# Batch 0's attention reordered by head halves in a fused pooled-attention and MLP kernel

## The chip, the cores and the metric

The kernel runs on one core of one Trainium2 chip. Its time is the device time of one launch in microseconds, as the median of several runs. The kernel before takes 300.92 us (three runs, 300.75 to 301.02). The profile is of one execution; its span, from the first to the last instruction, is 299.0 us.

## The reference

Eight batches of eight heads, 576 tokens and 64 values per head. Keys and values are averaged over groups of eight tokens, so that 72 pooled keys remain. The queries attend to these, and the result goes through a layer with `h - tanh(h)` between two weight matrices.

```python
# q, k, v: (8, 8, 576, 64) float32; w_in: (512, 2048); w_out: (2048, 512)
k_p = k.reshape(B, H, 72, 8, D).mean(axis=3)
v_p = v.reshape(B, H, 72, 8, D).mean(axis=3)
scores = scale * np.matmul(q, k_p.transpose(0, 1, 3, 2))
attn = softmax(scores)
attn_out = np.matmul(attn, v_p)                       # (8, 8, 576, 64)
x = attn_out.transpose(0, 2, 1, 3).reshape(4608, 512)
h = x @ w_in
return (h - np.tanh(h)) @ w_out                       # (4608, 512) float32
```

## The kernel before

The tokens of the second part are worked off in nine groups of 512. Group 0 needs only the first 512 tokens of batch 0. While TensorE works on a group, the other engines prepare the attention of the next batch. Two things are special at the start: nothing can be multiplied with the weights until batch 0's attention is there, and batch 1's attention is computed between the products of group 0.

Names: `k_raw`, `v_raw`, `v_bf` and `q_bf` are loaded or cast inputs; pooled keys of two heads (144 rows) fill one tile of 128 rows, and the 16 rows left over of each of the four pairs are collected in a fifth tile (index `NM`). `KB` holds the pooled keys turned, `qT` the queries turned, `E` the exponentials of the scores, `VB` the pooled values with a column for the denominator, `x0` and `xT` the attention result before and after turning, `gT` is `h - tanh(h)`.

The loads at the start, on three queues (SyncE, ScalarE, GpSimd):

```python
load_main(k_pairs, k_raw[0], 0, 0, 1)      # nc.sync
load_q0(0, 2)                              # nc.scalar
load_main(k_pairs, k_raw[0], 0, 1, 2)
load_q0(2, 4)
load_main(k_pairs, k_raw[0], 0, 2, 4)
load_q0(4, 8)
load_dense(k_pairs, k_raw[0], 0, nc.scalar)   # leftover keys
load_dense(v_pairs, v_raw[1], 0, nc.scalar)   # leftover values
warm_pe(9)                                    # products of zeros on TensorE
...
nc.gpsimd.memset(q_bf[64:128, R, :, :], 0.0)
... # mask
for i in range(2):
    nc.gpsimd.tensor_scalar_mul(VB[i][:, :, D:D1], mask[:, :, :], float(POOL))
nc.gpsimd.dma_start(out=v_bf[:, 0:NM, :], in_=v_pairs[0, 0:128, :, :])   # casts to bf16
... # spread
for c in range(4):
    load_w1(c)                                # casts to bf16
load_w2(0)
nc.gpsimd.tensor_copy(out=v_bf[:, NM, :], in_=v_raw[1][:, NM, :])
load_w2(1)
... # three memsets
after(load_k(1), w1_dmas[1])                  # starts when that quarter of w1 has landed
load_q(1, False)
load_main(v_pairs, v_raw[1], 1, 0, NM)
```

Batch 0's attention, in the order of TensorE's queue:

```python
pool_k(0, nc.vector, 0, 1)
pool_k(0, nc.vector, 1, 2)
q_turn(nc.scalar.copy, 0, 2)                  # cast of q to bf16
q_turn(nc.scalar.copy, 2, 4)
k_turn(0, 1)
q_pe_transpose(0, (0,), "act")
warm_pe(1)
k_turn(1, 2)
q_pe_transpose(0, (1,), "act")
warm_pe(2)
scores_wide(0, (0, 1))                        # product and exponential
...                                           # load of the last 64 queries
q_turn(nc.scalar.copy, 4, 6)
q_turn(nc.scalar.copy, 6, 8)
pool_k(0, nc.vector, 2, 4)
warm_pe(6)
k_turn(2, 4)
pool_k(0, nc.vector, NM, NT)                  # leftover keys
warm_pe(2)
q_pe_transpose(0, (2, 3), "act")
warm_pe(2)
scores_wide(0, (2, 3))
k_turn_left()
warm_pe(2)
v_ps = v_pe_pool(NM, NT, spread)              # values are pooled by TensorE
scores_wide(0, (NM,))
v_left(VB[0], v_ps[:, 0, :, :], nc.vector)
vs = v_pe_pool(0, NM, ident, 4)
v_main(VB[0], vs, nc.vector, 0, 2)
v_main(VB[0], vs, nc.vector, 2, 4)
...
warm_pe(2, b0=3)
av_pair(0, 0, 2)                              # token blocks 0, 1; heads 0 to 3
av_pair(1, 0, 5)                              # blocks 2, 3
av_pair(0, 1, 0)                              # heads 4 to 7
warm_pe(1)
x0_turn((0, 1), 0, 7, nc.scalar.copy)
av_pair(1, 1, 2)
warm_pe(1)
x0_turn((2, 3), 0, 5, nc.scalar.copy)
warm_pe(2)
h_open(3, 4)                                  # first half of the sum of one tile of h
x0_turn((0, 1), 1, 7, nc.scalar.copy)
h_open(0, 0)
h_open(1, 1)
x0_turn((2,), 1, 5, nc.scalar.copy)
x0_turn((3,), 1, 6, nc.vector.tensor_copy)
h_open(2, 2)
h_open(4, 3)
...
for i in range(5):
    mlp_h_mms(0, i, 2, 4)                     # second half of the sum
    mlp_h_act(i, gts)                         # tanh on ScalarE, h - tanh on VectorE
for i in range(5, NHID):                      # NHID = 16
    mlp_h(0, i, gts)
    ...                                       # i == 7, 9, 11, 13: the last 64 tokens of batch 0
pool_k(1, nc.gpsimd, mid=(2, 3))              # load_w2(2), load_w2(3) after the first addition
after(load_k(2), w2_dmas[2])
...
for u in range(16):
    mlp_o(0, u % 4, u // 4 * 4, u // 4 * 4 + 4, gts, o_pools[u % 4])   # four products with w2
    ...                                       # u == 2: turn batch 1's keys; u == 3: its queries
```

`av_pair` includes the normalization: a reciprocal and a product on VectorE.

Of the kernel before, what the change touches and what calls it, by code (L numbers as in the profile page):

```python
# [19 lines left out]
R = 4  # L20
# [17 lines left out]
def kernel(  # L38
# [41 lines left out]
    ps_h = Banks(0, 1, 2)  # L80
    ps_o = Banks(3, 4)
    ps_a = Banks(5, 6, 7)
# [25 lines left out]
    rot = [0]  # L108

    def ps_any(shape, dtype, name):  # L110
        pool, tag = [(ps_a, "ps_a"), (ps_h, "hT_ps")][rot[0] % 2]
        rot[0] += 1
        return pool.tile(shape, dtype, name=name, tag=tag)
# [40 lines left out]
    def load_q(b, tail=True):  # L154
        if b not in q_raws:
            q_raws[b] = raw.tile([128, H, R + 1, D], FP32, name="q_raw", tag="q_raw")
        t = q_raws[b]
        nc.sync.dma_start(
            out=t[:, :, 0:R, :], in_=q[b, :, 0:QA, :].rearrange("h (p j) d -> p h j d", j=R)
        )  # L160
        if tail:
            load_q_tail(b, t, nc.sync)

# [3 lines left out]
    def q_cast(b, eng=nc.gpsimd.tensor_copy, parts=1):  # L167
# [7 lines left out]
        eng(out=q_bf[:QT, R, :, :], in_=t[:QT, :, R, :])  # L175
# [75 lines left out]
    def v_main(vb, vs, eng, t0, t1):  # L251
# [3 lines left out]
            in0=vs[:, t0:t1, :, :].to_broadcast([128, n, 2, D]),  # L255
# [192 lines left out]
    def mlp_h_mms(g, i, f0, f1, pool=None):  # L448
# [3 lines left out]
        for fb in range(f0, f1):  # L452
# [5 lines left out]
                stop=(fb == NFB - 1),  # L458
            )
# [101 lines left out]

    nc.vector.memset(zeros, 0.0)  # L562
# [6 lines left out]
    load_main(k_pairs, k_raw[0], 0, 2, 4)  # L569
    load_q0(4, 8)  # L570
    load_dense(k_pairs, k_raw[0], 0, nc.scalar)
    load_dense(v_pairs, v_raw[1], 0, nc.scalar)

    warm_pe(9)
    nc.vector.memset(warm[:, :], 0.0)
    nc.scalar.activation(out=warm[:, :], in_=warm[:, :], func=ACT.Exp)
    nc.vector.memset(KB[0][:, :], 0.0)

    make_identity(nc, ident)
    nc.gpsimd.memset(q_bf[64:128, R, :, :], 0.0)  # L580
# [16 lines left out]
    for i in range(2):  # L597
        nc.gpsimd.tensor_scalar_mul(VB[i][:, :, D:D1], mask[:, :, :], float(POOL))
    nc.gpsimd.dma_start(out=v_bf[:, 0:NM, :], in_=v_pairs[0, 0:128, :, :])  # L599
# [5 lines left out]
    for c in range(4):  # L605
        load_w1(c)
    load_w2(0)
    nc.gpsimd.tensor_copy(out=v_bf[:, NM, :], in_=v_raw[1][:, NM, :])
    load_w2(1)
    nc.gpsimd.memset(k_raw[1][:, NM, :], 0.0)  # L610
    nc.gpsimd.memset(v_raw[0][:, NM, :], 0.0)
    nc.gpsimd.memset(KB[1][:, :], 0.0)

    q_raws[1] = raw.tile([128, H, R + 1, D], FP32, name="q_raw", tag="q_raw")
    after(load_k(1), w1_dmas[1])
    load_q(1, False)
    load_main(v_pairs, v_raw[1], 1, 0, NM)

    def k_turn(ta, tb):
        ps = ps_any([128, tb - ta, 128], FP32, "kT_ps")  # L620
        for t in range(ta, tb):
            turn_tile(ps[:, t - ta, :], kdups[0], t)
        kb_main(KB[0], ps, ta, tb, (nc.vector.tensor_copy, nc.vector.tensor_copy))

    def k_turn_left():
        ps = ps_any([128, 128], FP32, "kT_ps")
        turn_tile(ps[:, :], kdups[0], NM)
        kb_left(KB[0], ps, nc.vector.tensor_copy)

    pool_k(0, nc.vector, 0, 1)  # L630
    pool_k(0, nc.vector, 1, 2)
# [21 lines left out]

    q_turn(nc.scalar.copy, 0, 2)
    q_turn(nc.scalar.copy, 2, 4)
    k_turn(0, 1)
    q_pe_transpose(0, (0,), "act")
    warm_pe(1)
    k_turn(1, 2)
    q_pe_transpose(0, (1,), "act")  # L660
    warm_pe(2)
    scores_wide(0, (0, 1))
    nc.scalar.dma_start(out=t0[:QT, :, R, :], in_=q[0, :, QA:S, :].rearrange("h p d -> p h d"))
    q_turn(nc.scalar.copy, 4, 6)
    q_turn(nc.scalar.copy, 6, 8)
    pool_k(0, nc.vector, 2, 4)
    warm_pe(6)
    k_turn(2, 4)
    pool_k(0, nc.vector, NM, NT)
    warm_pe(2)  # L670
    q_pe_transpose(0, (2, 3), "act")
    warm_pe(2)
    scores_wide(0, (2, 3))
    k_turn_left()
    warm_pe(2)
    v_ps = v_pe_pool(NM, NT, spread)
    scores_wide(0, (NM,))
    v_left(VB[0], v_ps[:, 0, :, :], nc.vector)
    vs = v_pe_pool(0, NM, ident, 4)
    v_main(VB[0], vs, nc.vector, 0, 2)  # L680
    v_main(VB[0], vs, nc.vector, 2, 4)
    load_left(v_pairs, v_raw[1], 1, nc.scalar)
    load_q_tail(1, q_raws[1], nc.scalar)
    gts = []

    def av_pair(p, half, b0):
        ps = PS[:, b0 : b0 + 2, 0 : 4 * D1].rearrange("p k (h d) -> p k h d", d=D1)
        for k in range(2):
            av_mms(0, 2 * p + k, half, ps[:, k, :, :])
        rden = work.tile([128, 2, 4, 1], FP32, name="rden2", tag="rden2")  # L690
# [26 lines left out]
    def h_open(i, b0):  # L717
        mlp_h_mms(0, i, 0, 2, bank(b0, [128, TG]))

    warm_pe(2, b0=3)  # L720
    av_pair(0, 0, 2)
    av_pair(1, 0, 5)
    av_pair(0, 1, 0)
    warm_pe(1)
    x0_turn((0, 1), 0, 7, nc.scalar.copy)
    av_pair(1, 1, 2)
    warm_pe(1)
    x0_turn((2, 3), 0, 5, nc.scalar.copy)
    warm_pe(2)
    h_open(3, 4)  # L730
    x0_turn((0, 1), 1, 7, nc.scalar.copy)
    h_open(0, 0)
    h_open(1, 1)
    x0_turn((2,), 1, 5, nc.scalar.copy)
    x0_turn((3,), 1, 6, nc.vector.tensor_copy)
    h_open(2, 2)
    h_open(4, 3)
    ps_any = ps_b1
    ps_h.n = ps_o.n = 0
    nc.scalar.copy(out=q_bf[:QT, R, :, :], in_=t0[:QT, :, R, :])  # L740
    for i in range(5):
        mlp_h_mms(0, i, 2, 4)
        mlp_h_act(i, gts)


    for i in range(5, NHID):
        mlp_h(0, i, gts)
        if i == 7:
            q_pe_tail(0)
        if i == 9:  # L750
            scores_tail(0)
        if i == 11:
            x4 = av(0, 4, ps_any, False)
        if i == 13:
            x_pe_transpose(0, 4, x4)
    pool_k(1, nc.gpsimd, mid=(2, 3))
# [5 lines left out]
    for u in range(16):  # L762
        qd, tb = u // 4, u % 4
        mlp_o(0, tb, qd * 4, qd * 4 + 4, gts, o_pools[tb])
        if u == 0:
            q_cast(1, nc.scalar.copy, 2)
        if u == 2:
# [86 lines left out]
```

The softmax here doesn't subtract the row's maximum and nothing guards it: scores larger than these inputs give would overflow.

## Time and profile before

| | before |
|---|---|
| time, median of 3 | 300.92 us |
| span of the profile | 299.0 us |
| bytes moved | 49.79 MB, 167 GB/s |
| products with w2 (L481) | 560, 134.3 us busy |
| products with w1 (L453) | 576, 126.8 us busy |
| products of zeros (L550) | 30, 10.4 us busy |

A line such as the following is one group of instructions: line in the kernel, engine, operation, what is written from what, shapes, count, then busy time and mean duration in ns, then the idle time of the engine before them and what ended it.

```profile
L481 PE MATMUL PS<-w2b,gT 128*128 128x512 bf16 x560 | 134.3, 379 | 0.0
L453 PE MATMUL PS<-xT,w1b 128*128 128x512 bf16 x576 | 126.8, 379 | 0.6 <-ACT xT L712 0.6
L550 PE MATMUL PS<-xT 128*128 128x512 bf16 x30 | 10.4, 463 | 1.3 <-DVE xT L562 1.3
```

PE is TensorE, DVE VectorE, ACT ScalarE, POOL GpSimd, SP SyncE; a trailing q is the queue in which an engine issues its transfers. Products are pipelined, so that the mean duration of one is longer than the step from one to the next.

### The profile page before, as it was taken

What the parts mean: (1) busy time and instruction counts of PE and PEld (TensorE: products, weight loads), DVE (VectorE), ACT (ScalarE), POOL (GpSimd) and SP (SyncE); (2) the same over time, 40 slices, a digit from 0 to 9 for tenths busy, and PEclk for the clock granted to TensorE, in tenths of its full rate; (3) what the DMA queues carried; (4) which work ended last, traced back from release to release, by engine and by line L of the source; (5) the groups of instructions that cost most, each with busy time, mean ns of one, the idle gap of its engine ahead of it and who ended that gap; (6) DMA issues with size and microseconds to landing.
All of it is one profiled execution on the core that took longest, in us unless ns stands there. A gap on an engine that the chain in (4) does not pass through costs nothing.

```text
span 299.0 us, 4704 instructions
## 1 busy us (share of the span) xinstructions
PE 291.5 (97%) x1672; PEld 142.8 (48%) x1672; DVE 158.4 (53%) x336; ACT 148.8 (50%) x279; POOL 115.7 (39%) x110
## 2 busy tenths in 40 slices
PE   7999999999999999999999999999999999999994
PEld 3454355544544454445544554455445544444443
DVE  5658665673547444753476247715680758008600
ACT  4647583666146623664266416651666066126511
POOL 8600906770396109913971099208930000000000
PEclk9999999999999999999999999999999999999999
DMA  7999999749955995699648974895431630111033
GB/s 259 221 211 280 310 235 328 233 89 331 233 109 109 290 283 129 109 297 250 105 89 236 313 166 88 265 294 137 89 66 35 90 96 0 37 70 36 2 70 70
DMA packets 66183, 49.79 MB, mean 167 GB/s; under 512 B 39920, under 2 KB 52976, under 8 KB 66160
## 3 DMA queue, kind: packets, MB, share of 16 engines
q1 hardware_dynamic: 58832, 42.94, 55.5%
q0 software_dynamic: 4752, 4.72, 9.5%
q10 hardware_dynamic: 2576, 1.84, 2.2%
q8 instruction: 13, 0.21, 0.3%
q14 instruction: 10, 0.08, 0.1%
HBM read 36.70 MB, written 9.44 MB: 154 GB/s over the span
## 4 chain that ended last, share of the span: by engine, by line
PE 85%; DMA 9%; POOL 4%; issue 0%; SPq 0%; ACT 0%; DVE 0%; POOLq 0%; DVEq 0%
PE PS L481 40%; PE PS L453 37%; DMA w1b<-in_moe_w_in_dram 4%; PE PS L368 4%; DMA k_raw<-in_k_dram 4%; PE PS L321 3%; POOL k_raw L221 1%; DMA out_dram<-o_sb 1%; POOL k_raw L226 1%; POOL kd L229 1%; POOL w2b L535 0%; PE PS L416 0%; POOL v_raw L599 0%; PE PS L194 0%; POOL w1b L528 0%
## 5 line engine op out<-in xcount | busy, mean ns | idle before, releaser
L481 PE MATMUL PS<-w2b,gT 128*128 128x512 bf16 x560 | 134.3, 379 | 0.0
L466 DVE TENSOR_TENSOR gT<-PS,t_sb 128x512 bf16<-128x512 f32 x144 | 98.9, 691 | 56.9 <-ACT t_sb L464 56.7
L453 PE MATMUL PS<-xT,w1b 128*128 128x512 bf16 x576 | 126.8, 379 | 0.6 <-ACT xT L712 0.6
L464 ACT ACTIVATE t_sb<-PS 128x512 f32<-128x512 f32 x144 | 85.6, 597 | 38.5 <-PE PS L453 37.7
L453 PEld LDWEIGHTS <-w1b 128*128 128x128 bf16 x576 | 55.9, 98 | 67.3 <-issue 0.8
L481 PEld LDWEIGHTS <-gT 128*128 128x128 bf16 x560 | 52.5, 98 | 52.0 <-issue 1.4
L490 ACT COPY o_sb<-PS 128x512 f32<-128x512 f32 x33 | 19.3, 586 | 75.2 <-PE PS L481 75.2
L385 DVE RECIPROCAL rden<-PS 128x4 f32<-128x4 f32 x72 | 12.8, 177 | 52.6 <-PE PS L368 52.3
L171 POOL CAST q_bf<-q_raw 128x2048 bf16<-128x2048 f32 x6 | 11.3, 1890 | 60.2 <-issue 34.2
L386 DVE TENSOR_TENSOR x_sb<-PS,rden 128x256 bf16<-128x256 f32 x72 | 30.6, 424 | 2.9 <-DMA xT<-x_sb 0.4
L221 POOL TENSOR_TENSOR k_raw<-k_raw 128x1280 f32<-128x1280 f32 x7 | 20.2, 2887 | 26.5 <-DMA k_raw<-in_k_dram 26.5
L340 ACT ACTIVATE E<-PS 128x288 bf16<-128x288 f32 x60 | 21.4, 409 | 13.2 <-PE PS L321 13.0
L368 PEld LDWEIGHTS <-E 128*128 128x128 bf16 x240 | 16.8, 98 | 8.3 <-issue 0.4
L368 PE MATMUL PS<-VB,E 128*128 128x130 bf16 x240 | 20.2, 220 | 0.1
L239 POOL TENSOR_TENSOR v_raw<-v_raw 128x1280 f32<-128x1280 f32 x6 | 17.4, 2900 | 0.0
L321 PE MATMUL PS<-qT,KB 128*128 128x288 bf16 (+5 forms) x128 | 17.0, 289 | 0.2
L321 PEld LDWEIGHTS <-KB 128*128 128x128 bf16 (+1 forms) x128 | 7.0, 96 | 10.2 <-issue 3.5
L550 PE MATMUL PS<-xT 128*128 128x512 bf16 x30 | 10.4, 463 | 1.3 <-DVE xT L562 1.3
L229 POOL TENSOR_TENSOR kd<-k_raw 128x640 bf16<-128x640 f32 x7 | 10.8, 1539 | 0.5
L226 POOL TENSOR_TENSOR k_raw<-k_raw 128x640 f32<-128x640 f32 x7 | 10.8, 1542 | 0.5
L242 POOL TENSOR_TENSOR v_raw<-v_raw 128x640 f32<-128x640 f32 x6 | 9.2, 1538 | 0.5
L272 POOL COPY KB<-kT 64x288 bf16<-64x288 bf16 x6 | 2.5, 418 | 13.8 <-DMA kT<-kd 13.8
(78 smaller groups left out, 107.1 us busy)
## 6 DMA issues: line engine op xcount, KB each, us to landing
k_raw<-in_k_dram SPq DMA_DIRECT2D x7, 1024.0 KB, 5.9
q_raw<-in_q_dram SPq DMA_DIRECT2D x7, 1024.0 KB, 10.2
v_raw<-in_v_dram SPq DMA_DIRECT2D x7, 1024.0 KB, 9.2
out_dram<-o_sb SPq DMA_DIRECT2D x38, 128.0 KB, 2.4
out_dram<-o_sb SPq DMA_DIRECT2D x16, 256.0 KB, 2.8
w1b<-in_moe_w_in_dram POOLq DMA_DIRECT2D x4, 512.0 KB, 13.7
w2b<-in_moe_w_out_dram POOLq DMA_DIRECT2D x4, 512.0 KB, 16.8
k_raw<-in_k_dram SPq DMA_DIRECT2D x7, 128.0 KB, 5.9
```

What stands on the lines that cost most here:

```text
L221: first = eng.tensor_tensor(out=r[:, :, 0:4, :], in0=r[:, :, 0:4, :], in1=r[:, :, 4:8, :], op=ALU.add)
L226: eng.tensor_tensor(out=r[:, :, 0:2, :], in0=r[:, :, 0:2, :], in1=r[:, :, 2:4, :], op=ALU.add)
L239: eng.tensor_tensor(out=r[:, :, 0:4, :], in0=r[:, :, 0:4, :], in1=r[:, :, 4:8, :], op=ALU.add)
L321: nc.tensor.matmul(dst[p : p + w], lhsT=KB[b % 2][:, o : o + w], rhs=qTs[b][:, m, c0:c1], start=True, stop=True,)
L340: nc.scalar.activation(out=E[:, t, half * hs : (half + 1) * hs], in_=ps[:, :], func=ACT.Exp, scale=SCALE)
L368: nc.tensor.matmul(ps[:, 2 * n : 2 * n + 2, :].rearrange("p h d -> p (h d)") if n < 2 else ps.rearrange("p (a s) d -> p a s d", s=2)[:, :, ...
L386: nc.vector.tensor_tensor(out=x_sb[:, half, :, :], in0=ps[:, :, 0:D], in1=rden[:, :, :].to_broadcast([128, 4, D]), op=ALU.mult,)
L453: nc.tensor.matmul(h_tiles[i][:, :], lhsT=w1b[:, fb, i * 128 : (i + 1) * 128], rhs=xT[:, fb, tok0 : tok0 + TG], start=(fb == 0), stop=(fb ...
L464: nc.scalar.activation(out=t_sb[:, :], in_=h_ps[:, :], func=ACT.Tanh)
L466: nc.vector.tensor_sub(out=gT[:, :], in0=h_ps[:, :], in1=t_sb[:, :])
L481: nc.tensor.matmul(o_ps[:, :], lhsT=gts[i][:, tb * 128 : (tb + 1) * 128], rhs=w2b[:, i, :], start=(i == 0), stop=(i == NHID - 1),)
L490: (nc.vector.tensor_copy if g == 0 and tb % 2 else nc.scalar.copy)(out=o_sb[:, :], in_=o_ps[:, :])
```

## The change

Batch 0's attention is arranged in two halves of the heads. The products of the first half (heads 0 to 3) need the scores of tiles 0, 1 and half of the leftover tile only, and v's first two tiles; they are put ahead of the scores of tile 3. For this v is loaded in two parts, the leftover scores are taken in two halves with an exponential each, and v is pooled in two parts. The leftover keys are loaded on SyncE's queue ahead of key tiles 2 and 3, and pooled on GpSimd; a quarter of q's cast goes to GpSimd. Most products of zeros are left out. Tiles of h are opened on half the columns as soon as two blocks are there. The loads of batch 1 are spread: each waits for a quarter of a weight matrix. The third and fourth quarter of w2 are issued after the pooling of batch 1's keys.

```diff
-    ps_h = Banks(0, 1, 2)
-    ps_o = Banks(3, 4)
-    ps_a = Banks(5, 6, 7)
+    ps_h = Banks(3, 5, 2)
+    ps_o = Banks(4, 1)
+    ps_a = Banks(0, 6, 7)
...
     load_q0(2, 4)
-    load_main(k_pairs, k_raw[0], 0, 2, 4)
+    load_dense(k_pairs, k_raw[0], 0)
     load_q0(4, 8)
-    load_dense(k_pairs, k_raw[0], 0, nc.scalar)
+    load_main(k_pairs, k_raw[0], 0, 2, NM)
     load_dense(v_pairs, v_raw[1], 0, nc.scalar)
...
     make_identity(nc, ident)
-    nc.gpsimd.memset(q_bf[64:128, R, :, :], 0.0)
...
-    for i in range(2):
-        nc.gpsimd.tensor_scalar_mul(VB[i][:, :, D:D1], mask[:, :, :], float(POOL))
-    nc.gpsimd.dma_start(out=v_bf[:, 0:NM, :], in_=v_pairs[0, 0:128, :, :])
+    nc.gpsimd.tensor_scalar_mul(VB[0][:, :, D:D1], mask[:, :, :], float(POOL))
+    load_v0(0, 2)
+    load_v0(2, NM)
+    load_w1(0)
...
-    for c in range(4):
-        load_w1(c)
-    load_w2(0)
-    nc.gpsimd.tensor_copy(out=v_bf[:, NM, :], in_=v_raw[1][:, NM, :])
-    load_w2(1)
...
-    after(load_k(1), w1_dmas[1])
-    load_q(1, False)
-    load_main(v_pairs, v_raw[1], 1, 0, NM)
+    pool_k(0, nc.gpsimd, NM, NT)
+    load_w1(1)
...
+    k_turn(0, 1, 0)
     q_pe_transpose(0, (0,), "act")
-    warm_pe(1)
-    k_turn(1, 2)
+    warm_pe(1, b0=7)
+    k_turn(1, 2, 2)
     q_pe_transpose(0, (1,), "act")
-    warm_pe(2)
-    scores_wide(0, (0, 1))
+    warm_pe(1, b0=7)
+    score_main(0, 4)
+    score_main(1, 5)
+    warm_pe(3, b0=7)
     q_turn(nc.scalar.copy, 4, 6)
-    q_turn(nc.scalar.copy, 6, 8)
+    q_turn(nc.gpsimd.tensor_copy, 6, 8)
+    nc.gpsimd.tensor_copy(out=v_bf[:, NM, :], in_=v_raw[1][:, NM, :])
+    load_w1(2)
+    load_w1(3)
+    load_w2(0)
+    ... # a scaling and four memsets on GpSimd
+    load_left(v_pairs, v_raw[1], 1, nc.gpsimd)
+    load_q_tail(1, q_raws[1], nc.gpsimd)
+    load_w2(1)
     pool_k(0, nc.vector, 2, 4)
-    warm_pe(6)
-    k_turn(2, 4)
-    pool_k(0, nc.vector, NM, NT)
-    ... # the order of before, above
+    k_turn_left(6)
+    q_pe_transpose(0, (2,), "act")
+    k_turn(2, 4, 0)
+    score_left(0, 1)
+    score_main(2, 7)
+    q_pe_transpose(0, (3,), "act")
+    va = v_pe_pool(0, 2, ident, 2)
+    v_main(VB[0], va, nc.vector, 0, 2)
+    v_ps = v_pe_pool(NM, NT, spread, 3)
     v_left(VB[0], v_ps[:, 0, :, :], nc.vector)
...
+    after([ld], w1_dmas[0])                                   # the last 64 queries of batch 0
+    after([load_main(k_pairs, k_raw[1], 1, 0, NM)], w1_dmas[1])
+    load_dense(k_pairs, k_raw[1], 1)
+    after([load_q(1, False)], w1_dmas[3])
+    after([load_main(v_pairs, v_raw[1], 1, 0, NM)], w2_dmas[0])
...
     av_pair(0, 0, 2)
-    ... # the order of before, above
+    av_norm(0, 0, 2)
+    av_pair(1, 0, 4)
+    score_main(3, 0)
+    score_left(1, 1)
+    vc = v_pe_pool(2, NM, ident, 7)
+    v_main(VB[0], vc, nc.vector, 2, NM, 2)
+    av_norm(1, 0, 4)
+    x0_turn((0, 1), 0, 2, nc.scalar.copy)
     av_pair(0, 1, 0)
+    av_norm(0, 1, 0)
+    x0_turn((2, 3), 0, 4, nc.scalar.copy)
+    av_pair(1, 1, 6)
+    av_norm(1, 1, 6)
+    h_open(0, 3, 0, 256)                                      # columns 0 to 255
+    h_open(1, 5, 0, 256)
+    h_open(0, 3, 256, 512)
+    x0_turn((0, 1), 1, 0, nc.scalar.copy)
+    h_open(1, 5, 256, 512)
+    h_open(2, 2, 0, 512)
+    x0_turn((2,), 1, 6, nc.scalar.copy)
+    x0_turn((3,), 1, 7, nc.vector.tensor_copy)
+    h_open(3, 4, 0, 512)
...
-    for i in range(5):
+    for i in range(4):
         mlp_h_mms(0, i, 2, 4)
         mlp_h_act(i, gts)
...
-    for i in range(5, NHID):
+    for i in range(4, NHID):
         mlp_h(0, i, gts)
... # the last 64 tokens of batch 0 at i == 6, 9, 11, 13; their turn at u == 0
-    pool_k(1, nc.gpsimd, mid=(2, 3))
+    pool_k(1, nc.gpsimd)
+    load_w2(2)
+    load_w2(3)
     after(load_k(2), w2_dmas[2])
...
         if u == 0:
+            x_pe_transpose(0, 4, x4)
             q_cast(1, nc.scalar.copy, 2)
         if u == 2:
+            nc.scalar.copy(out=q_bf[:QT, R, :, :], in_=q1_raw[:QT, :, R, :])
             k_transpose(1, ps_any, (nc.vector.tensor_copy, nc.vector.tensor_copy))
```

## The prediction

> **What bounds the kernel now.** I read the page's table of busy times first, to see whether there is one bound or several.
>
> ```profile
> PE 291.5 (97%) x1672; PEld 142.8 (48%) x1672; DVE 158.4 (53%) x336; ACT 148.8 (50%) x279; POOL 115.7 (39%) x110
> ```
>
> TensorE is busy for 97% of the span. A change can only take away what TensorE does not need: the start, before it can multiply with the weights, and holes after that. The change touches nothing after batch 1's attention, so the next view is the chain of waits over the first 60 us (start, duration, what).
>
> ```profile
> 5.87 12.56 DMA w1b<-in_moe_w_in_dram
> 18.45 0.38 SPq L125
> 18.93 10.97 DMA k_raw<-in_k_dram
> ...
> 30.06 2.90 POOL k_raw L221
> 32.96 1.48 POOL w2b L535 x2
> 34.45 1.58 POOL k_raw L226
> 36.09 1.55 POOL kd L229
> 37.69 0.45 PE PS L282 x5
> ```
>
> The reader is to see one hole here: batch 1's keys start to load only when the second quarter of w1 has landed (18.45), land near 30, are pooled on GpSimd with 1.48 us of w2 issues in between, and TensorE gets them at 37.69. From there on the chain is TensorE without a break to 291.7. The start itself stands in the timeline (start, duration, engine, line, operation, shapes, in brackets the idle time before and what ended it).
>
> ```profile
> 10.46 0.89 POOL L608 CAST v_raw<-v_raw 128x512 bf16<-128x512 f32 x1 [1.61 <-DVE KB L273]
> ...
> 10.91 0.58 DVE L226 TENSOR_TENSOR k_raw<-k_raw 128x128 f32<-128x128 f32 x1
> ...
> 13.03 1.05 PE L642 MATMUL PS<-v_raw,ident 128*128 128x256 bf16 x8
> ...
> 14.60 1.20 PE L368 MATMUL PS<-VB,E 128*128 128x130 bf16 x18
> ...
> 17.90 0.69 DVE L692 TENSOR_TENSOR x<-PS,rden 128x512 bf16<-128x512 f32 x1
> 18.35 0.59 PE L453 MATMUL PS<-xT,w1b 128*128 128x512 bf16 x2 [0.55 <-ACT xT L712]
> ...
> 20.09 4.26 PE L453 MATMUL PS<-xT,w1b 128*128 128x512 bf16 x19
> ```
>
> The attention products start near 14.6, the last normalization ends at 18.59, the first product with w1 starts at 18.35, and from 20.09 such products run close together. Between 18.35 and 20.09 six of them (three tiles of h, half each) and eight small turns fill TensorE. So "20.09 with six done" is the mark that the change has to beat. One such product takes 13.81 us / 64 = 0.216 us in the undisturbed group from 85.83 us on (the chain has "13.81" for each group of 64).
>
> **What the Trainium skill says.** Three pages bear on the steps below, and one on a rival.
> "SBUF — State Buffer", section "SBUF: two separate sides", says that VectorE and GpSimd share a pair of ports, which one of them holds for a whole instruction when GpSimd works and VectorE reads two operands from SBUF. The trace agrees: the 128x128 addition at 10.91 took 0.58 us while the GpSimd cast ran from 10.46, and its twins took 0.29.
> "GPSIMD Engine Reference", section 3.1, puts GpSimd's addition at about twice VectorE's time. The trace agrees: 128x1280 takes 2.89 us on GpSimd and 1.49 on VectorE.
> "DMA: Bandwidth & Descriptors", section "Queues, rings and completion order", says that a DMA engine goes round the queues that have work. The trace agrees in part: from 25 to 31 us GpSimd's queue took 63% and SyncE's 51%, but from 6 to 9 us ScalarE's queue took 76% and GpSimd's only 16%.
>
> **The change part by part.**
> (a) Loads. The leftover keys (128 KB) go to the SyncE queue ahead of key tiles 2 and 3, v goes in two loads, and GpSimd reaches the first of them earlier: one memset (0.52) and one scaling (0.28) fewer stand before it, so it is issued at about 3.69 - 0.80 = 2.9. Key tiles 2 and 3 landed at 7.8; 128 KB at the 375 GB/s of 3 to 6 us is 0.35, so I put them at 8.2. v landed at 12.0 (3.69 + 8.3); its first half should land near 10.3, as its queue gets little before 9.
> (b) Engine work. VectorE loses the pooling of the leftover keys (0.43 + 0.58 + 0.29 = 1.3 us). GpSimd gets it, at my estimate of twice 0.43 + 0.29 + 0.29, so 2.0 at most, and gets one q cast (0.61 on ScalarE; 0.9 like its v cast). ScalarE loses that 0.61 and gets one exponential more (0.60, as the leftover scores go in two halves): nothing net.
> (c) Warm-up products. 9+1+2+6+2+2+2+2+1+1+2 = 30 become 9+1+1+3 = 14. They stood in TensorE's queue in front of real work: six of them at 7.96 took 1.46 us. But most filled waits.
> (d) The attention chain, step by step with the durations above. Key tiles 2 and 3 are pooled on VectorE by 8.2 + 0.69 + 0.42 + 0.43 = 9.8 without port conflicts; the GpSimd cast of q (0.9) can block one of these additions, so 10.7 with one. Turning them and copying to KB (0.25 + 0.30 + 0.28, and gaps) gives 11.7; the scores and exponential of tile 2 lie beside the pooling of v on TensorE (0.5 for the first half, as two of four tiles of 1.05; 0.40 for the leftovers) and two VectorE products (0.43 each). The first attention product then starts at about 13.4, with 13.1 and 13.8 as the ends I could argue for, against 14.6 now.
> From there VectorE sets the pace: four normalizations of 0.21 + 0.69 and one v product of 0.43 in between that waits for TensorE's second half of v (0.45 lost). From 13.75 (one pair of products after the start) this is 13.75 + 0.9 + 0.45 + 0.43 + 2.7 = 18.2 for the last one, against 18.59. The first half of the heads is turned by then, and h tiles 0 and 1 start on the first 256 columns near 17.1.
> By the same count TensorE has three h tiles half done (six products) and is about to do the turns at 18.6; the turns, 0.22, and the fourth tile follow. That is 20.09 - 18.8 = 1.3 us ahead of the mark. With the ends above, 0.8 to 1.6. I take 1.2.
> (e) Given back in the h stage. Four tiles are opened and not five, and tile 4 reuses bank 3, which tile 0 must have left: tanh 0.60 and subtraction 0.69 plus gaps, 1.5 us after its last product. TensorE is back there after 4 x 0.43 = 1.7, less the 0.43 of tile 0 itself: it waits some 0.25. VectorE at 0.69 per tile and TensorE at 0.86 then run clear of each other. Cost 0.3.
> (f) The hole at 37. Before, TensorE has done its first twelve products with w2 at 36.99 and starts on keys at 37.69: 0.7 us. After, GpSimd pools batch 1's keys without the 1.48 us of issues, and its loads of q and v stand further back, so k has less beside it. If the second quarter of w1 lands at 18.1 and k needs 10.3 again, the keys are pooled at 28.4 + 2.90 + 1.58 + 1.55 = 34.4. TensorE wants them at 36.99 - 0.9 = 36.1. The hole closes: 0.7 gained. The turn of block 4, for which TensorE idled 0.32 us before 32.44, moves into the w2 stage and costs no wait: 0.3 gained.
> Sum: 1.2 - 0.3 + 0.7 + 0.3 = 1.9 us. 300.9 - 1.9 = 299.0. I add 0.2 for what the rivals weigh: 299.2.
>
> **The rivals.**
> First, port conflicts set the start. GpSimd casts q and v and pools keys just when VectorE pools tiles 2 and 3 (8 to 11 us); each conflict costs up to 0.9, and TensorE's order puts everything after that turn. Two conflicts instead of one make the start gain 0.3 in place of 1.2: 300.0. The 0.58 us addition speaks for it; that VectorE has 1.3 us less to do there speaks against.
> Second, the clock of TensorE. "TensorE: Matmul & The Clock Gate", Part 1, says that it falls to half after some 3.4 us without work. The trace has the other half: the first nine wide products take 4.02 us, 0.43 each at their pace, later ones 0.216. With 16 warm-ups fewer, TensorE has gaps from 9 to 17 us, though I find none over about 1 us. If it did fall, products from 17 on at half rate for 3.4 us would cost 1.7: 300.9 or a little more. One in ten.
> Third, weights become the wait. The last two quarters of w2 are issued only after batch 1's keys are pooled (34.4, not 32.9). They took 8.6 and 10.4 us to land; 34.4 + 8.6 is 43.0, and the ninth group of w2 products started at 44.37 before, about 42.5 now. This would give back 0.5: 299.7. With less q and v traffic left by then it could land by 41; I hold it for one in four.
> Fourth, nothing is left of the start because loads bound it anyway. The first quarter of w1 landed at 15.3 (5.19 + 10.1), well before 17; this speaks against it.
>
> **Range and chances.** With all steps right, 298.6 to 299.2; with the first or third rival 299.7 to 300.0; with two together 300.8. The start better than 1.6 and no cost in (e) gives 298.0. So 298.0 to 300.7 for eight in ten. Two per cent are 6 us; the whole start up to 18.35 with the hole is what could move, and no rival adds or takes 6 us: within 2% at 0.98, and 0.01 on each side.
>
> **What will show it.** (a) v's first load at about 2.9 us. (d) The first attention product near 13.4 and the first product with w1 near 17.1; later than 18.4 and the step is wrong. (b) VectorE's additions on tiles 2 and 3 at 0.69, 0.42, 0.43 mean no port conflict; one near 1.3 means one. (e) A TensorE wait for the subtraction before the fifth h tile. (f) The batch 1 key turn without idle time before it, and the w2 products between 40 and 46 without a wait for a DMA. Group 1's first product, now at 54.91, should come at 53.0 to 53.4; from there to the end the two traces should be alike. If the start gains and group 1 does not come earlier, (f) was wrong; wide products in the 17 to 22 us stretch at 0.43 would mean the clock.

## The result, and the profile after

The changed kernel takes 303.74 us (median of 4 runs, 303.24 to 304.19), the kernel before 300.97 (4 runs beside them, 300.75 to 301.03). The ratio is 1.0086, with a 95% interval of 1.0068 to 1.0103: slower by about 2.6 us, where the prediction had a gain of 1.7.

The first line to compare is that of busy times on the page of the changed kernel.

```profile
PE 288.3 (96%) x1638; PEld 143.1 (47%) x1668; DVE 158.4 (53%) x334; ACT 148.9 (49%) x279; POOL 121.3 (40%) x120
```

TensorE is busy for 3.2 us less than before (291.5) and the span is 2.5 us longer (301.5 against 299.0). So TensorE did not get more to do; it waits more. Where, the chain of waits over the first 30 us says (start, duration, what).

```profile
2.32 0.13 SPq L132
2.45 0.04 issue
2.49 9.20 DMA k_raw<-in_k_dram
11.69 0.02 issue
11.71 0.70 DVE k_raw L221
12.41 0.02 issue
12.44 0.72 DVE k_raw L226
13.16 0.02 issue
13.18 0.73 DVE kd L229
...
24.51 0.62 PE PS L453 x2
```

Before, the chain started with GpSimd's issues and the first weights. Now it starts with one load: key tiles 2 and 3 are issued at 2.49 us and are there only 9.20 us later, at 11.7. The prediction had them at 8.2. The timeline of the changed kernel shows what waited for them (start, duration, engine, line, operation, shapes, in brackets the idle time before and what ended it).

```profile
8.59 0.72 POOL L221 TENSOR_TENSOR k_raw<-k_raw 128x256 f32<-128x256 f32 x1 [2.91 <-DMA k_raw<-in_k_dram]
...
10.43 0.23 PE L282 MATMUL PS<-ident,kd 128*128 128x128 bf16 x1 [1.81 <-POOL kd L229]
...
11.71 0.69 DVE L221 TENSOR_TENSOR k_raw<-k_raw 128x512 f32<-128x512 f32 x1 [4.62 <-DMA k_raw<-in_k_dram]
12.07 0.62 ACT L619 CAST q_bf<-q_raw 128x512 bf16<-128x512 f32 x1 [3.46 <-DMA q_raw<-in_q_dram]
12.10 0.77 POOL L619 CAST q_bf<-q_raw 128x512 bf16<-128x512 f32 x1 [1.00 <-DMA q_raw<-in_q_dram]
12.44 0.71 DVE L226 TENSOR_TENSOR k_raw<-k_raw 128x256 f32<-128x256 f32 x1
12.74 0.61 PE L194 MATMUL PS<-ident,q_bf 128*128 128x128 bf16 x4 [2.08 <-ACT q_bf L619]
...
17.52 1.40 PE L368 MATMUL PS<-VB,E 128*128 128x130 bf16 x12 [0.17 <-DVE VB L253]
...
22.02 0.87 PE L754 MATMUL PS<-xT,w1b 128*128 128x256 bf16 x6
...
23.82 0.59 PE L754 MATMUL PS<-xT,w1b 128*128 128x512 bf16 x2
```

VectorE stands idle for 4.62 us until tiles 2 and 3 come, ScalarE for 3.46 us until heads 4 to 7 of q come. The leftover keys land first: GpSimd pools them from 8.59 on and TensorE turns them at 10.43, but what stands next in TensorE's queue are the turns of q's next heads and of tiles 2 and 3. Attention's first product comes at 17.52 (before 14.60), the first with w1 at 22.02 (before 18.35). The line at 23.82 is the prediction's mark, six half tiles done and the turns behind it: before 20.09. Before, tiles 2 and 3 were used at 7.83:

```profile
7.83 0.69 DVE L221 TENSOR_TENSOR k_raw<-k_raw 128x512 f32<-128x512 f32 x1 [0.49 <-DMA k_raw<-in_k_dram]
```

TensorE's clock shows in the table by stages (stage, length, busy time and number on TensorE, weight loads, VectorE, ScalarE, GpSimd, then granted clock, DMA share, GB/s). Of the changed kernel:

```profile
9.00:12.00 3.00, 0.23 (x1) 0.10 (x1) 0.29 (x1) 0.00 (x0) 1.94 (x4) 0.94 1.19 238
12.00:15.00 3.00, 1.54 (x8) 0.57 (x8) 2.63 (x6) 1.27 (x3) 2.90 (x4) 0.50 1.24 207
15.00:18.00 3.00, 2.73 (x24) 2.18 (x25) 0.86 (x2) 1.60 (x3) 2.80 (x7) 0.50 1.25 207
```

Before, the middle one:

```profile
12.00:15.00 3.00, 2.91 (x33) 1.91 (x32) 1.41 (x4) 1.22 (x3) 1.61 (x4) 1.00 1.21 196
```

TensorE worked 0.23 us of the three from 9 to 12, and its clock is half from there to 18; before it was 1.00 in all three stages. The four turns at 12.74 take 0.61 us, where four take 0.39 at 23.60.

Cut at two places of TensorE's work, the two traces divide like this (us):

| | before | changed | difference |
|---|---|---|---|
| start of the span to the mark | 20.09 | 23.82 | +3.73 |
| mark to group 1's first product | 34.78 (to 54.87) | 33.82 (to 57.64) | -0.96 |
| group 1's first product to the end | 244.1 | 243.9 | -0.2 |

Group 1's first products, before and changed:

```profile
54.87 3.83 PE L453 MATMUL PS<-xT,w1b 128*128 128x512 bf16 x17
57.64 1.24 PE L453 MATMUL PS<-xT,w1b 128*128 128x512 bf16 x5
```

So the start lost 3.7, and behind it 1.0 came back: the chain has batch 1's key turn (L282) right behind the products with w2, where before there was a hole.

```profile
38.91 1.73 PE PS L482 x8
40.64 0.28 PE PS L282 x5
40.92 0.22 PE PS L482
```

### The profile page after: what moved, and what is told of

Read it like the earlier page. It is cut to its first block, busy times and chain, and to the rows that moved or that the text cites. A ratio compares the mean times of both kernels' runs of the same rounds, so it can differ in the third digit from the quotient of the medians.

```text
span 301.5 us, 4682 instructions
## 1 busy us (share of the span) xinstructions
PE 288.3 (96%) x1638; PEld 143.1 (47%) x1668; DVE 158.4 (53%) x334; ACT 148.9 (49%) x279; POOL 121.3 (40%) x120
## 4 chain that ended last, share of the span: by engine, by line
PE 91%; DMA 4%; DVE 3%; issue 1%; ACT 0%; SPq 0%; DVEq 0%
PE PS L453 40%; PE PS L482 40%; PE PS L368 5%; PE PS L321 4%; DMA k_raw<-in_k_dram 3%; DMA out_dram<-o_sb 1%; PE PS L628 0%; PE PS L194 0%; PE PS L754 0%; PE PS L416 0%; PE PS L737 0%; DVE VB L253 0%; DVE kd L229 0%; DVE k_raw L226 0%; DVE x L725 0%
## 5 line engine op out<-in xcount | busy, mean ns | idle before, releaser
L482 PE MATMUL PS<-w2b,gT 128*128 128x512 bf16 x542 | 132.2, 379 | 1.2 <-issue 0.3
L453 PE MATMUL PS<-xT,w1b 128*128 128x512 bf16 x557 | 124.1, 379 | 0.8
L453 PEld LDWEIGHTS <-w1b 128*128 128x128 bf16 x568 | 55.2, 98 | 66.8 <-DVE xT L745 0.6
L221 POOL TENSOR_TENSOR k_raw<-k_raw 128x1280 f32<-128x1280 f32 (+1 forms) x8 | 20.9, 2615 | 24.9 <-DMA k_raw<-in_k_dram 12.9
L321 PE MATMUL PS<-qT,KB 128*128 128x288 bf16 (+5 forms) x128 | 17.8, 294 | 0.4 <-ACT qT L117 0.2
L321 PEld LDWEIGHTS <-KB 128*32 128x32 bf16 (+1 forms) x128 | 7.1, 96 | 10.9 <-issue 3.6
L229 POOL TENSOR_TENSOR kd<-k_raw 128x640 bf16<-128x640 f32 (+1 forms) x8 | 11.2, 1401 | 0.6
L226 POOL TENSOR_TENSOR k_raw<-k_raw 128x640 f32<-128x640 f32 (+1 forms) x8 | 11.2, 1400 | 0.6
```

What stands on the lines that cost most here:

```text
L221: first = eng.tensor_tensor(out=r[:, :, 0:4, :], in0=r[:, :, 0:4, :], in1=r[:, :, 4:8, :], op=ALU.add)
L321: nc.tensor.matmul(dst[p : p + w], lhsT=KB[b % 2][:, o : o + w], rhs=qTs[b][:, m, c0:c1], start=True, stop=True,)
L453: nc.tensor.matmul(h_tiles[i][:, :], lhsT=w1b[:, fb, i * 128 : (i + 1) * 128], rhs=xT[:, fb, tok0 : tok0 + TG], start=(fb == 0), stop=(fb ...
L482: nc.tensor.matmul(o_ps[:, :], lhsT=gts[i][:, tb * 128 : (tb + 1) * 128], rhs=w2b[:, i, :], start=(i == 0), stop=(i == NHID - 1),)
```

## The experiments

The question is what made the start 5.0 us later than predicted (23.82 against 18.8). Three theories: **the loads** (the new order of issue put tiles 2 and 3 behind q's last heads, and v, issued a microsecond earlier, takes a part of what is left); **the clock** (fewer products of zeros let it fall); **the order of the work** (keys pooled on GpSimd, conflicts with VectorE, the products in halves). A second question came up on the way: why repairing the start does not bring a gain. Each run below has the kernel before beside it on the same chip; ratios are to that one. "Changed kernel" and "kernel before" name the one that was edited.

### 1. Two key loads exchanged

Changed kernel; the leftover keys go back behind tiles 2 and 3 on SyncE's queue, nothing else.

```diff
-    load_dense(k_pairs, k_raw[0], 0)
-    load_q0(4, 8)
     load_main(k_pairs, k_raw[0], 0, 2, NM)
+    load_q0(4, 8)
+    load_dense(k_pairs, k_raw[0], 0)
```

> Only the leftover keys and key tiles 2 and 3 change places on SyncE's queue. Theory 'queue order' (tiles 2 and 3 were issued 0.8 us later than before and so fell behind q's heads 4 to 7): tiles 2 and 3 land at 8 to 9 in place of 11.7, TensorE's clock stays full or nearly so, and the time falls from 303.7 to 300 to 301. Rival 'early v' (v's transfers, begun at 7.2 and not 8.2, take the share of k and q): tiles 2 and 3 improve little, to 10 or 11, and the time stays above 302.5. Rival 'new order of work is slow by itself': landing early, but the time stays above 302.5.

Measured: 301.95 us, ratio 1.0028 (1.0015 to 1.0040). Tiles 2 and 3 are used at 8.98, heads 4 to 7 of q only at 11.76; attention's first product is at 16.43, group 1 at 56.89. About two thirds of the loss goes by this one exchange. What remains hangs on q and the clock: with the tiles there 2.7 us earlier, attention starts only 1.1 earlier, and at half clock (0.50 from 12 to 18), so that the mark (23.08) comes 0.7 earlier.

### 2. v issued as late as before

Changed kernel; a memset and a scaling go back in front of v's loads on GpSimd, so they are issued at 3.69 and not at 2.65.

```diff
     make_identity(nc, ident)
+    nc.gpsimd.memset(q_bf[64:128, R, :, :], 0.0)
...
-    nc.gpsimd.tensor_scalar_mul(VB[0][:, :, D:D1], mask[:, :, :], float(POOL))
+    for i in range(2):
+        nc.gpsimd.tensor_scalar_mul(VB[i][:, :, D:D1], mask[:, :, :], float(POOL))
     load_v0(0, 2)
```

> Only GpSimd's order changes: the memset of q_bf and the second scaling stand ahead of v's loads again, so that v's packets begin near 8.2 in place of 7.2. Theory 'queue order': tiles 2 and 3 still begin at 6.0 and land at 9.5 to 11, the time falls by at most 1, to 302.7 to 303.7. Rival 'early v': tiles 2 and 3 and q land at 8.5 to 9.5 and the time falls to 301 or below.

Measured: 302.64 us, 1.0060 (1.0041 to 1.0079). Tiles 2 and 3 at 10.31, q at 10.36, attention at 16.11, group 1 at 56.97. Issuing a microsecond later a transfer that nothing waits for then is worth about 1.1 us, though the intervals of the two kernels overlap a little.

### 3. The clock held up by products of zeros

Changed kernel; 21 wide products of zeros in the waits, loads as they are.

```diff
     pool_k(0, nc.vector, 2, 4)
+    warm_pe(8, b0=7)
     k_turn_left(6)
+    warm_pe(9, b0=7)
     q_pe_transpose(0, (2,), "act")
+    warm_pe(2, b0=7)
     k_turn(2, 4, 0)
     score_left(0, 1)
+    warm_pe(2, b0=7)
     score_main(2, 7)
```

> The loads stay as in the changed kernel; 21 products of zeros fill TensorE's waits between 8.6 and 15 us. Theory 'half the loss is the clock': the granted clock is 1.00 in every stretch, tiles 2 and 3 land at 11.7 as before, and the time falls by 1.3 to 2.0, to 301.7 to 302.4. Rival 'the clock costs nothing, as the stretch waits for data and VectorE': within 0.4 of 303.7.

Measured: 303.22 us, 1.0068 (1.0041 to 1.0095). The table by stages of this run:

```profile
9.00:12.00 3.00, 2.65 (x14) 1.05 (x12) 1.03 (x2) 0.62 (x1) 2.84 (x5) 1.00 1.19 235
12.00:15.00 3.00, 2.27 (x15) 1.05 (x14) 2.02 (x5) 0.77 (x2) 3.00 (x5) 1.00 1.25 207
15.00:18.00 3.00, 2.59 (x36) 1.85 (x34) 1.25 (x5) 1.48 (x3) 2.80 (x7) 1.00 1.24 207
```

The clock is 1.00 in all three, and group 1 comes at 56.58, 1.06 earlier. Not all of that is the clock: in this profile tiles 2 and 3 are used at 10.94 and q is cast at 10.65, 0.8 and 1.4 earlier than in the changed kernel, though issued alike. Cleaner is the stretch from attention's first product to the mark: 5.97 us here (16.79 to 22.76), 6.30 in the changed kernel. So the clock costs between 0.3 and 1.1 us; it is real and the smaller part. The time falls by 0.5 only, and the intervals overlap: in group 1 two steps from one product to the next are 1.02 us (to 72.92, for batch 2's keys) and 0.61 us (to 88.58, for a transfer of x_sb) where 0.216 is usual, and the group lasts 32.00 in place of 30.80. That was the first sign of the second question.

### 4 and 5. Both load edits; both and warm

Changed kernel with the edits of 1 and 2; then the same with 12 products of zeros.

```diff
+    warm_pe(6, b0=7)
     k_turn_left(6)
+    warm_pe(3, b0=7)
     q_pe_transpose(0, (2,), "act")
+    warm_pe(1, b0=7)
     k_turn(2, 4, 0)
     score_left(0, 1)
+    warm_pe(2, b0=7)
     score_main(2, 7)
```

> Both edits of the loads together, nothing else. Theory 'late loads are all of it': tiles 2 and 3 land at 7.8 and q at 9, as in the kernel before, the clock stays at 1.00, and the time is that of the prediction, 298.6 to 300.0. Rival 'new order of work is slow by itself': loads as before, but the time at or above 300.9.

> Both edits of the loads and 12 products of zeros in TensorE's waits from 8.6 to 14. Clock theory: granted clock 1.00 in every stretch, first products with w1 at full pace 0.5 to 1.0 us earlier than with the loads alone (21.5), runs closer together than 300.4 to 304.8. With the wait for batch 2's keys behind it, the time does not fall as much: 300.5 to 301.5. If that wait is nothing, 299.9.

Measured: 302.32 us, 1.0047 (1.0025 to 1.0069), and 302.02, 1.0041 (1.0020 to 1.0061). Their single times spread from 300.43 to 304.80 and from 300.56 to 304.67. In the profiled executions (301.37 and 300.56) tiles 2 and 3 are used at 8.21 and 7.61, the mark is at 20.80 and 21.09, group 1 at 54.62 and 54.92. So with the loads repaired 2.7 to 3.0 of the 3.7 us are back, in these executions; that the medians don't show it goes with the spread (last section) and with group 1, which lasted 31.90 in the first. In run 5 the clock is 1.00 throughout and the mark is still no earlier than in run 4: products of zeros lie on its chain, with 0.65, 0.38 and 0.54 us.

### 6. The order of loads alone, in the kernel before

Kernel before; only the order of three loads is that of the change. All 30 products of zeros, v late, keys pooled on VectorE.

```diff
-    load_main(k_pairs, k_raw[0], 0, 2, 4)
+    load_dense(k_pairs, k_raw[0], 0)
     load_q0(4, 8)
-    load_dense(k_pairs, k_raw[0], 0, nc.scalar)
+    load_main(k_pairs, k_raw[0], 0, 2, 4)
```

> The kernel before, with the leftover keys third on SyncE's queue and tiles 2 and 3 behind them, and nothing else of the change. Theory 'queue order': tiles 2 and 3 land at 9 to 10.5 and not 7.8, q's heads 4 to 7 near 9, TensorE's clock stays full as its products of zeros are all there, and the time rises by 0.5 to 2, to 301.5 to 303. Rival 'the order matters only together with the early v': within 0.4 of before.

Measured: 303.44 us, 1.0074 (1.0043 to 1.0105): as slow as the changed kernel. Its timeline:

```profile
10.47 0.69 DVE L221 TENSOR_TENSOR k_raw<-k_raw 128x512 f32<-128x512 f32 x1 [3.27 <-DMA k_raw<-in_k_dram]
...
12.42 0.39 PE L282 MATMUL PS<-ident,kd 128*128 128x128 bf16 x2 [3.02 <-DVE kd L229]
...
18.48 1.20 PE L368 MATMUL PS<-VB,E 128*128 128x130 bf16 x18
```

Tiles 2 and 3 come at 10.47, attention at 18.48, group 1 at 57.56 (changed kernel 57.64). Its clock is 0.51 from 12 to 15 us, with all products of zeros in place: they stand in TensorE's queue behind the turn that waits. So the order of these three loads is enough for a loss of this size, in a kernel that has nothing else of the change. The loss is a little more than expected, and the clock falls, against the expectation: here it follows from the waiting, as no product of zeros is missing.

### 7. Half the products of zeros, in the kernel before

Kernel before, 14 in place of 30.

```diff
-    warm_pe(6)
+    warm_pe(2)
     k_turn(2, 4)
     pool_k(0, nc.vector, NM, NT)
-    warm_pe(2)
     q_pe_transpose(0, (2, 3), "act")
... # ten more left out in the same way
```

> The kernel before with 14 products of zeros in place of 30, as many as the changed kernel has, and nothing else. Theory 'the clock falls only because the loads are late': with tiles 2 and 3 at 7.8 the clock stays at 1.00 or dips for under 2 us, and the time is within 0.6 of before. Rival 'too few products of zeros drop the clock by themselves': granted clock at 0.5 for 3 us or more between 10 and 20, and the time 0.8 to 2 more than before.

Measured: 301.08 us, 1.0004 (0.9993 to 1.0015); clock 1.00, group 1 at 55.09. In the old order of work, with data in time, half the products of zeros are enough to keep the clock up.

### 8. The new order of work behind the old loads

Changed kernel with all loads as before (leftover keys on ScalarE's queue behind q, v late), leftover keys pooled on VectorE, TensorE's order adapted to that.

```diff
-    load_dense(k_pairs, k_raw[0], 0)
-    load_q0(4, 8)
     load_main(k_pairs, k_raw[0], 0, 2, NM)
+    load_q0(4, 8)
+    load_dense(k_pairs, k_raw[0], 0, nc.scalar)
...
-    pool_k(0, nc.gpsimd, NM, NT)
...
-    k_turn_left(6)
+    warm_pe(4, b0=1)
     q_pe_transpose(0, (2,), "act")
     k_turn(2, 4, 0)
-    score_left(0, 1)
-    score_main(2, 7)
+    pool_k(0, nc.vector, NM, NT)
... # leftover turn and scores behind tile 2's scores
```

> The new order of the attention with the loads of before in full: leftover keys on ScalarE's queue behind q and pooled on VectorE, v issued where it was, 7 products of zeros in the waits. If step (d) of the prediction was right apart from the loads: tiles 2 and 3 at 7.9, q's heads 4 to 7 at 9.0, first attention product at 13.0 to 13.8, products with w1 at full pace from 19.3, group 1 at 53.5. Then the wait for batch 2's keys (ready near 70.5) takes 1 to 2 back: 299.8 to 300.8. Rival 'new order is slow by itself': full pace later than 20.5.

Measured: 301.69 us, 1.0015 (0.9999 to 1.0032). Tiles at 7.58, q at 8.81, attention at 14.12, but the mark at 21.43 and group 1 at 55.24; the clock was 0.51 from 15 to 18. With before's loads the new order is level with before and not ahead of it. Data was in time here, and 21 products of zeros stood in the queue, 7 more than in the changed kernel; the clock fell all the same. From attention's first product to the mark it took 7.31 us, and 5.76 at full clock in run 12 below, which has three such products more and pools the leftover v earlier. So in the new order the clock can cost some 1.5 us even when data is in time.

### 9. The later part of the change alone

Kernel before with the prediction's step (f): batch 1's keys pooled without the w2 issues in between, block 4's turn moved. It was profiled twice, the second time in a single execution.

```diff
-        if i == 13:
-            x_pe_transpose(0, 4, x4)
-    pool_k(1, nc.gpsimd, mid=(2, 3))
+    pool_k(1, nc.gpsimd)
+    load_w2(2)
+    load_w2(3)
...
         if u == 0:
+            x_pe_transpose(0, 4, x4)
```

> The kernel before with step (f) alone: batch 1's keys are pooled without the w2 issues in between, which come after it, and block 4 is turned in the w2 stage. If (f) was right as predicted: the hole of 0.7 before the key turn closes, group 1 starts at 53.9 and the time falls by 1.0, to 299.9. Theory 'the hole moves': group 1 starts at 53.9 too, but the third quarter of w2 lands 3 us later, so batch 2's keys load and get placed 3 us later, near 71, TensorE waits for them at 70, and the time is that of before or up to 0.7 more.

> A second profile of the kernel before with step (f) alone. In the first one tiles 2 and 3 landed at 9.5 and not 7.8, with the same loads as before. If that was chance of one execution, they land at 7.6 to 8.2 here, group 1 starts at 53.8 to 54.2, and TensorE waits for batch 2's keys at 70 all the same.

Measured: 301.51 us, 1.0016 (0.9996 to 1.0037), and 300.85 in the single execution. In the first profile tiles 2 and 3 came at 9.48, though its loads are those of before, so it says little. In the second they came at 7.69 and the mark at 19.98, and its chain reads:

```profile
53.85 0.12 PE PS L416 x4
53.97 7.46 PE PS L453 x34
...
80.23 1.43 PE PS L481 x7
81.65 4.00 DMA xT<-x_sb
85.66 0.14 issue
85.79 3.18 PE PS L453 x14
```

Group 1 starts at 53.93 in place of 54.87: 0.94 gained, as step (f) had it. TensorE does not wait for batch 2's keys at 70, as was expected. But before group 2 it waits for a transfer of x_sb of 4.00 us, and group 2 starts at 85.79, where before it started at 85.67. All of it is given back, one group later. In this run the last two quarters of w2 are issued at 36.00 (before 32.91), batch 2's keys at 42.17 (41.57), these are pooled from 50.33 (47.66) and placed by 69.5 (68.0).

### 10. w2 issued earlier

The kernel of 9 with both w2 loads issued near the start of the span, behind the second quarter.

```diff
     nc.gpsimd.memset(KB[1][:, :], 0.0)
+    load_w2(2)
+    load_w2(3)
...
     pool_k(1, nc.gpsimd)
-    load_w2(2)
-    load_w2(3)
```

> The kernel before with step (f), but the third and fourth quarter of w2 are issued early, right behind the second, and not after batch 1's keys are pooled. Theory 'the hole moves because w2 came late': the key turn no longer waits, the third quarter lands at or before 41.6, batch 2's keys are in place by 68 and nothing waits at 70; the time is 299.6 to 300.2. Rival 'transfers are the bound': v of batch 1 lands late instead and its attention waits near 46, no gain, 300.6 or more.

Measured: 302.31 us, 1.0053 (1.0038 to 1.0067). Batch 1's v now lands at 45.4 (before 40.35), TensorE is idle for 1.54 us before 40.69, waiting for q, and group 1 is at 57.44. Some 1.5 us of that lie in the start: in this profile tiles 2 and 3 came at 9.47 and the mark at 21.56. At neither place was the megabyte of w2 free; what changed was who waits.

### 11 to 13. The best of both, and q ahead of v

Run 8 with the leftover v pooled earlier and more products of zeros; the same with batch 2's q loaded before its v; and the kernel of 9 with q before v.

```diff
     score_main(2, 7)
+    v_ps = v_pe_pool(NM, NT, spread, 4)
+    warm_pe(1, b0=1)
     k_turn_left(2)
...
     after(load_k(2), w2_dmas[2])
-    load_v(2)
     load_q(2)
+    load_v(2)
```

> The new order with the loads of before in full, and the pooling of the leftover values put ahead of the leftover keys' turn on TensorE, two more products of zeros. If the new order costs nothing by itself once data and clock are right: first attention product at 13.4 to 13.8, clock 1.00 throughout, turns of the last two blocks with six products done at 18.8 to 19.2 (5.4 after the start, as predicted), time 299.6 to 300.3. If the order itself is longer: the same start, but 6.1 to 6.5 from the start to that mark (19.6 to 20.2), time 300.4 to 301.

> As the run before, and batch 2's q is loaded ahead of its v. If batch 2's preparation is what eats an earlier start: q of batch 2 is cast 0.5 to 1 us sooner after its keys are pooled, no wait in groups 1 and 2, and 0.3 to 0.8 less than the run before. If nothing waits there: within 0.3 of it.

> The kernel before with step (f) and batch 2's q ahead of its v. If the given-back 1.07 us in group 1 comes from batch 2's chain on GpSimd and SyncE, the wait before group 2 falls from 1.3 to 0.5 or less and the time is 300.0 to 300.5, below before. Rival 'the transfers of x wait for the loads of batch 3 whatever their order': 300.8 or more.

Measured: 301.75 us, 1.0014 (0.9996 to 1.0032); 301.52, 1.0001 (0.9983 to 1.0020); 301.30, 0.9999 (0.9983 to 1.0014). The second one's profile has the loads in time and the clock at 0.999, so it shows the new order of work with nothing late at the start:

```profile
14.30 0.85 PE L368 MATMUL PS<-VB,E 128*128 128x130 bf16 x12 [0.15 <-DVE VB L253]
...
18.26 0.87 PE L759 MATMUL PS<-xT,w1b 128*128 128x256 bf16 x6
...
20.06 0.59 PE L759 MATMUL PS<-xT,w1b 128*128 128x512 bf16 x2
```

Attention's first product is 0.3 ahead of before (14.60), the mark level with it (20.06 against 20.09). None of the three medians is ahead of the kernel before. Their fastest executions are a little ahead of its fastest (300.21, 300.28 and 300.07, against 300.55), and their slowest behind its slowest (303.70, 302.86 and 303.24, against 302.52); no profile caught one of the fastest. That q goes ahead of v makes no clear difference: run 12 is within the noise of run 11, and in run 13's profile TensorE is still idle for 0.57 us before group 2, waiting for x_sb.

## Why the prediction was wrong

**Step (a), the loads, failed.** It worked out "128 KB at the 375 GB/s of 3 to 6 us is 0.35, so I put them at 8.2". That counts the bytes ahead of a load. Measured, tiles 2 and 3 came at 11.7, 3.5 later. They were issued at 2.49 in place of 1.73, behind the leftover keys (1.77) on SyncE's queue, and now also behind q's heads 4 to 7 (1.83) on ScalarE's. The DMA view of 4.5 to 6.0 us shows what followed (queue, packets, MB, share of 16 engines; q1 is SyncE's, q10 ScalarE's). Before:

```profile
q1 hardware_dynamic: 166, 0.33, 59.8%
q10 hardware_dynamic: 243, 0.23, 44.1%
```

Changed:

```profile
q10 hardware_dynamic: 481, 0.48, 93.7%
q1 hardware_dynamic: 9, 0.01, 1.6%
```

In the changed kernel SyncE's queue hardly moves in this stretch; in runs 2 and 6, which have the same order, it has 9.5% and 11.5%. From 6.0 us on it moves beside ScalarE's, and from 7.18 on v's transfers, which began at 8.21 before, take a share too. Tiles 2 and 3 land at 11.7, q's heads 4 to 7 at 12.0. Run 6 shows that the order does it, run 1 undoes most of it, run 2 shows v's part.

Why SyncE's queue stands still is not shown. Order of issue is one reading. The other is that the leftover load, now at the head of that queue, holds it: it takes 0.68 us to issue, the loads of key tiles 0.39 to 0.58, and it was issued ahead of q's heads 4 to 7 and still landed at 8.5 only. No run separates the two. In the Trainium skill, "DMA: Bandwidth & Descriptors", section "Queues, rings and completion order", an engine goes round the queues that have work. From 4.5 to 6.0 us the trace shows nothing of that (93.7% against 1.6%), but no view tells whether SyncE's queue had packets ready.

The step also put the first half of v near 10.3; it landed at 11.9. The 16% of GpSimd's queue from 6 to 9 us, from which the prediction read that it gets little, was no sharing: its first packets moved at 8.21.

**Step (d) left out two loads and was too short.** It starts the chain at tiles 2 and 3 alone. Attention also needs q's heads 4 to 7 and the leftover keys, whose turn stands ahead of that of tiles 2 and 3 in TensorE's queue; when these land was not asked. The chain of run 1 goes through q:

```profile
1.83 9.91 DMA q_raw<-in_q_dram
11.76 0.63 ACT q_bf L619
```

In run 4, where tiles 2 and 3 are used at 8.21, TensorE waits for the leftover keys from GpSimd:

```profile
10.84 0.23 PE L282 MATMUL PS<-ident,kd 128*128 128x128 bf16 x1 [2.07 <-POOL kd L229]
```

In the profiles below attention's first product comes 4.7 to 5.6 us after the cast of q's heads 4 to 7 begins (6.1 in run 3, 7.9 in run 6), whatever tiles 2 and 3 do:

| kernel | tiles 2, 3 used | q heads 4 to 7 cast | first attention product |
|---|---|---|---|
| before | 7.83 | 8.98 | 14.60 |
| changed | 11.71 | 12.07 | 17.52 |
| run 1 | 8.98 | 11.76 | 16.43 |
| run 4 | 8.21 | 10.01 | 14.71 |
| run 8 | 7.58 | 8.81 | 14.12 |
| run 12 (the second of 11 to 13) | 7.68 | 9.25 | 14.30 |

No profile reaches 13.4; the earliest is 14.12. With tiles 2 and 3 in time, in runs 8 and 12, which pool the leftover keys on VectorE, it takes 6.5 to 6.6 us from them to this product, where the step had 5.2. From that product to the mark the step had 5.4 us; it is 5.76 to 5.97 in the four runs with a full clock (3, 5, 11, 12) and 6.30 in the changed kernel. The predicted lead of 1.2 at the mark is 0.0 in run 12, with everything in time.

The 5.0 us between 18.8 and 23.82 divide so: 3.5 because tiles 2 and 3 came at 11.7 and not at 8.2; 0.6 from there to attention's first product (5.8 in place of 5.2); 0.9 from it to the mark (6.3 in place of 5.4), of which 0.3 to 0.5 goes with the clock and the rest with the order of the work.

**The rivals.** The second, the clock, came true behind the late data, at 0.3 to 1.1 us in the changed kernel and not 1.7. Products left out are not its cause in the old order (runs 6 and 7); in the new order, run 8 lost some 1.5 us to it with data in time. The prediction looked for one long gap; the trace has idle times of 1.81 and 2.08 us with 0.23 of work between. In the Trainium skill, "TensorE: Matmul & The Clock Gate", Part 1, has the clock fall to half after an idle window of some 3.4 us. The changed kernel agrees if little work counts like none. Run 8 does not agree: TensorE was busy for 2.45 us of the three from 12 to 15, its longest recorded idle time since 9 us was 0.95, and the clock fell near 14.5. What the clock follows stays open. The first, conflicts of ports, is there and small: the additions at 12.44 and 13.18 took 0.71 and 0.72 beside GpSimd casts, where 0.42 and 0.43 are usual, so two of 0.3 each. The fourth argued from w1 that loads don't bound the start; the loads that did bound it were those of keys and q.

**Step (e)** was not measured by itself. With (f) it makes the second row of the table of differences: predicted 0.7 together, measured 0.96, and the same 33.82 or 33.83 us from mark to group 1 in the changed kernel and in runs 4 and 5.

**Step (f) was right in mechanism and size in the kernel before**, 0.94 in the second profile of 9. In the changed kernel its hole closed by luck. The step had batch 1's keys landed at 28.4 and pooled at 34.4; they landed at 32.2 and were pooled at 38.4:

```profile
36.85 1.53 POOL L229 TENSOR_TENSOR kd<-k_raw 128x640 bf16<-128x640 f32 x1
```

TensorE came for them at 40.64, because the start was late. With the predicted mark of 18.8 and the same 16.8 us from the mark to this turn it would have come at 35.6 and waited for 2.8 us (an estimate from these times). Where the mark is early, such waits appear. In run 12 (mark at 20.06) TensorE is idle for 0.25 us for the keys and then waits for batch 1's q, whose load starts only when the last quarter of w1 has landed:

```profile
24.64 13.07 DMA q_raw<-in_q_dram
...
40.78 0.38 PE PS L321
```

There it takes 35.16 us from the mark to group 1, 1.3 more than the 33.82 above. So the spread loads of batch 1 eat up part of an earlier start.

What also failed is "from there to the end the two traces should be alike", where group 1 is not late. Group 2's first product tells it:

| kernel | mark | group 1 | group 2 | span |
|---|---|---|---|---|
| before | 20.09 | 54.87 | 85.67 | 299.0 |
| changed | 23.82 | 57.64 | 88.44 | 301.5 |
| run 4 | 20.80 | 54.62 | 86.52 | 299.6 |
| run 5 | 21.09 | 54.92 | 85.72 | 298.8 |
| run 9, second profile | 19.98 | 53.93 | 85.79 | 299.1 |
| run 12 | 20.06 | 55.22 | 86.03 | 299.1 |

No profile has group 2 ahead of 85.67. The two that have group 1 ahead of 54.87 wait within it: run 4 for batch 2's keys and for x_sb's transfers, run 9 for the latter. Runs 3, 11, 13 and the first profile of 9 wait there too, with group 1 later, so an early group 1 is not the only reason. The third rival came near this: it asked whether the products with w2 wait for w2, and not what becomes of the transfers issued behind it, batch 2's. That the whole chain from w2's issue to batch 2 is what holds group 2 is argued from its times in run 9 and fits run 10; no run took it away, so it is not shown. Why the transfer of x_sb takes 4.00 us stays open too.

**The range** had no room for this, because its worst case added rivals of 0.5 to 1.7 us to a load time that was taken as sure.

## What to carry to other kernels

What a load costs the ones behind it is not its bytes over the bandwidth: the order of three loads, which the prediction counted as 128 KB and 0.35 us, made the kernel before 2.2 us slower by itself. Before moving one, list all loads of the first microseconds by time of issue over all queues, and ask of each consumer which of its loads lands last. A transfer that nobody waits for yet still takes its share from one that is waited for, so issuing it earlier is no free gain. A wait that disappears because everything before it is late has not been removed. And a microsecond won in one group counts only if the next group's data is ready a microsecond earlier too; look one consumer further before adding it up.

## What the runs showed that was not expected

From 4.5 to 6.0 us of the changed kernel ScalarE's queue had 93.7% of the engines' time and SyncE's 1.6%, although loads were issued on both. In all three kernels with the leftover load ahead of tiles 2 and 3 SyncE's share is low there (1.6%, 9.5% and 11.5%); in the kernel before it is 59.8%.

GpSimd's queue moves its first packets some 4.5 us after the issue: 3.69 to 8.21 before, 2.65 to 7.18 in the changed kernel.

Kernels whose loads and times of issue in the first 4 us are those of before (v in one part or in two) landed tiles 2 and 3 at 7.6 to 7.8 us in some profiles (before, 7, 8, the second of 9, 12) and at 9.1 to 9.5 in others (the first of 9, 10, 11, 13). The counts of packets show that in the late ones the last few of SyncE's queue trail on to 8.5 us, when GpSimd's queue has begun. The late ones took 302.09 to 303.57 us, the early ones of the runs 300.85 to 300.93, and the times of one kernel spread over 2 to 4 us. What decides it is open. It also means that a shift of a microsecond or two between two single profiles says little by itself. The effect of the order of loads rests on times: the five of run 6 are 301.87 to 305.06, the 44 of the kernel before beside it 300.54 to 302.25.
